# A spectral layer's filter loaded in long rows, with the columns kept in natural order by a strided matmul read, and another order of the first loads

## The chip, the cores and the metric

The kernel runs on one core of one Trainium2 chip, in one launch. The metric is the device time of an execution in microseconds (us), a median over runs. All arithmetic on the matrix engine (TensorE, PE in the profile) is in bf16 with f32 sums.

## What is computed

The input x is 2048 x 512 (bf16). The first half of the layer is a spectral filter, the second a token-mixing MLP:

```python
X  = rfft2(layernorm(x))                 # over both axes: 2048 x 257 complex
h  = x + irfft2(X * (w_r + 1j * w_i))    # w_r, w_i: 2048 x 257 each
g  = layernorm(layernorm(h))             # over the 512 columns
u  = gelu(einsum("sd,sf->df", g, w1) + b1)      # w1: 2048 x 1376
out = h + transpose(einsum("df,fs->ds", u, w2) + b2)
```

## The kernel before, in words

Token n is 16 * n1 + n2: n1 lies on the 128 partitions, n2 counts 16 tiles of 128 x 512. Both Fourier transforms are done as matmuls, the long one in two factors (128 and 16). The stages, with the names that the profile shows:

1. **Head and f1.** x is loaded in pieces (tile `X`), and the 16 slices of the first DFT factor, `FP`, in four pieces. Each x tile gets its mean and variance: tiles 1 and 3 by two passes on ScalarE (ACT; `JK<-X` in the profile, `nm` and `bv` on GpSimd, then `rs` on ACT), the others by `bn_stats` on VectorE (DVE, line 655), then `rs` on ACT. `fs_op` (lines 629 to 636) scales a slice of `FP` by `rs` into `FS`; GpSimd (POOL) does nine of them, ACT three, DVE four. 64 matmuls `ps<-FS,X` follow; their results are copied to `Y`, 13 by ACT and 3 by DVE (lines 692 to 696). 20 filler matmuls on zeros (`warm`, line 623) stand at the start of PE and 12 more between these.
2. **The filter.** Eight units u = 0..7. In each, eight `f2` matmuls (`ps<-EM,Y`, the DFT over the 512 columns), two copies to `CS` on ACT, eight `x` matmuls (`ps<-CS,EM`, the 16-point factor, in two row halves of 64), then on DVE one multiply by the filter (`V<-ps,W`, line 741; in units 0 and 7 two halves), then 16 `g1` matmuls (`ps<-EM,V`) and two copies to `PQ` on ACT. In `g1` V is the stationary operand, which PE loads (LDWEIGHTS, "PEld" in the profile), and a constant moves.
3. **Back.** `g2` and `g3` matmuls per x tile, then DVE adds x (lines 792, 794, 801) and normalises (`HH`, line 806); the first W1 matmuls run in between.
4. **MLP.** W1 matmuls, gelu on ACT, W2 matmuls (line 829, whose weight loads read every 16th column of W2), final add on DVE and stores.

The `W` tile holds the two filters for 32 groups of columns' frequencies: on each partition, `[group, w_r or w_i, 257]`. A partition is numbered by `_row`: four rows, two signs by two components (real and imaginary part), for each of 32 residues. Both components need the same filter row, and the row of the negative sign runs through the groups in falling order.

The 256 columns that stage 2 treats are frequencies 1 to 256, and `f2` makes the odd ones (par 0) and the even ones (par 1) as two blocks of 128. Before the change these blocks stay apart through `x`, and the multiply reads W with a step of two elements to match them; `g1` then takes `V[:, g, w, par * NP:par * NP + NP]`.

The order on each engine is not written out by hand: every operation is given to `K.op` with its engine, an estimated duration and a priority, and `Builder.schedule` places the ready operation that can start earliest. The resulting order of each engine is fixed at build time; at run time semaphores hold an instruction until what it needs is there. `schedule` also has a small model of the landing times of DMAs (lines 331 to 334), which the change alters, so orders can move on several engines. Loads are issued by SyncE (SP) on one queue, some by ACT on its own. The loads of W come in three parts, for unit 0, units 1 to 3 and units 4 to 7 (lines 583 to 600); a V multiply waits for all the loads of its part. The loads of W1 wait until the last part of W has landed.

Two small things belong to the order of the first loads before the change: a DMA of 64 bytes (`touch`) as the first one on ACT's queue, and a memset (`gate`) that the load of FP piece 0 waits for.

Of the kernel before, what the change touches and what calls it, by code (L numbers as in the profile page):

```python
# [34 lines left out]


def _row(sign, comp, k2, s):
    return 4 * (k2 * 2 + s) + 2 * sign + comp


def _fwd_matrices(special):
# [133 lines left out]
class Builder:  # L175
# [101 lines left out]
    def schedule(self):  # L277
        ops = self.ops
        eng_free = {s: 0.0 for s in _STREAMS}
        dma_free = 0.0  # L280
        bank_unit = [None] * PSUM_BANKS
        bank_free = [0.0] * PSUM_BANKS
        bank_last = [[] for _ in range(PSUM_BANKS)]
        open_cls = {}
        remaining = {o.idx: len(o.deps) for o in ops}
        inner = {o.idx: sum(1 for d, _ in o.deps if d.unit is not None and d.unit is o.unit) for o in ops}
        for o in ops:
            o.dep_ready = 0.0
        ready = [o for o in ops if remaining[o.idx] == 0]
        streams = {s: [] for s in _STREAMS}  # L290
        order = []
        while len(order) < len(ops):
            best = None
            for o in ready:
                bank, avail = None, 0.0
                u = o.unit
                if u is not None and not u.claimed:
                    if not o.first or open_cls.get(u.cls, 0) >= self.limits.get(u.cls, 8):
                        continue
                    if not u.early and any(remaining[x.idx] > inner[x.idx] for x in u.ops if x.pw):  # L300
                        continue
                    cand = None
                    for b in range(PSUM_BANKS - u.nbanks + 1):
                        if all(bank_unit[i] is None for i in range(b, b + u.nbanks)):
                            t = max(bank_free[b:b + u.nbanks])
                            if cand is None or t < cand[0]:
                                cand = (t, b)
                    if cand is None:
                        continue
                    avail, bank = cand  # L310
                st = max(eng_free[o.stream], o.dep_ready, avail, o.not_before)
                key = (st, -o.prio, o.idx)
                if best is None or key < best[0]:
                    best = (key, o, st, bank)
            assert best is not None, [(o.name) for o in ready][:20]
            _, o, st, bank = best
            e = o.stream
            ready.remove(o)
            o.sched, o.start = True, st
            if not o.is_dma:  # L320
                o.lane = e
            if bank is not None:
                u = o.unit
                u.claimed, u.bank = True, bank
                open_cls[u.cls] = open_cls.get(u.cls, 0) + 1
                for b in range(bank, bank + u.nbanks):
                    bank_unit[b] = u
                    for prev in bank_last[b]:
                        o.deps.append((prev, True))
            eng_free[e] = st + o.occ  # L330
            if o.is_dma:
                x0 = max(st + (1750.0 if st < 900.0 else 2200.0), dma_free)
                dma_free = x0 + o.bytes / (min(o.rate, 310.0) if x0 < 7000.0 else o.rate)
                o.finish = dma_free + 200.0
            else:
                o.finish = st + o.lat
            streams[e].append(o)
            order.append(o)
            if o.unit is not None and o.last:
                u = o.unit  # L340
                open_cls[u.cls] -= 1
                for b in range(u.bank, u.bank + u.nbanks):
                    bank_unit[b] = None
                    bank_free[b] = o.finish
                    bank_last[b] = [x for x in u.ops if x.pr]
            for c in o.consumers:
                if c.sched:
                    continue
                need = any(d is o and n for d, n in c.deps)
                c.dep_ready = max(c.dep_ready, o.finish if need else st + o.occ)  # L350
                remaining[c.idx] -= 1
                if remaining[c.idx] == 0:
                    ready.append(c)
        self.order, self.streams = order, streams
# [68 lines left out]
def memory_layout():  # L423
# [23 lines left out]
    add("CS", [NP, 16, 2, 2, NP], bf, rd)  # L447
    add("H", [NP, NS2, D_LEN], bf, rd)
    rw = region(2 * NG * LW * 2)
    add("W", [NP, NG, 2, LW], bf, rw)  # L450
    add("HH", [NP, NS2, D_LEN], bf, rw)
    rv = region(32768)
    add("V", [NP, NG, 2, 256], bf, rv)
# [16 lines left out]
    add("ZT", [NP, D_LEN], bf, region(1024))  # L470
    add("bv", [NP, NS2], f32, region(64))
    add("tb", [NP, 8], f32, region(32))
    add("pt", [NP, 32], bf, region(64))
    add("B1s", [NP, 16], bf, region(32))
    add("B1f", [NP, 16], f32, region(64))
    add("B2s", [NP, NS2], bf, region(32))
# [15 lines left out]
def build_kernel(nc, A_x, A_w_r, A_w_i, B_w1, B_b1, B_w2, B_b2, out):  # L492
# [65 lines left out]
    def ldx(a, b, pr_):  # L558
        dma(f"ld_x{a}", X[:, a:b, :], x_psd[:, a:b, :], (b - a) << 17, outs=[X[:, a:b, :]], prio=pr_)

    def ldf(q, pr_, stream="sp", nb=0.0, after=()):
        sl = slice(4 * q, 4 * q + 4)
        dma(f"ld_FP{q}", FP[:, sl, :, :], cin["FP"][:, sl, :, :], 1 << 18, outs=[FP[:, sl, :, :]], prio=pr_, stream=stream, not_before=nb, after=after)

    ZT, BV = T["ZT"], T["bv"]
    K.op("zt", "dve", lambda eng, bank: eng.memset(ZT[:, :], 0.0), outs=[ZT[:, :]], occ=200.0, prio=60)  # L566
    gate = K.op("gate", "dve", lambda eng, bank: eng.memset(T["TT0"][:, :, :], 0.0), outs=[T["TT0"][:, :, :]], occ=560.0, prio=59)
    for q, (a, b) in enumerate(((0, 1), (1, 2), (2, 4), (4, 6))):
        ldx(a, b, 96 - q)
    ldf(1, 88)  # L570
    ldx(6, 8, 87)
    ldx(8, 10, 86)
    ldx(10, 12, 85)
    ldf(2, 84)
    ldx(12, 16, 83)
    ldf(3, 82)
    act("table", T["tb"][:, 0:1], EPS[:, 0:1], ACT.Abs_reciprocal_sqrt, 1, ins=[EPS[:, 0:1]], prio=95)
    dma("touch", T["pt"][0:1, :], cin["FP"][0:1, 0, 0, 0:32], 64, outs=[T["pt"][0:1, :]], prio=99, stream="act")
    ldf(0, 90, "act", after=[gate])
    dma("ld_E", EM[:, 0:1024], cin["EM"][:, 0:1024], 1 << 18, outs=[EM[:, 0:1024]], prio=44)  # L580
    dma("ld_MR", EM[:, 1024:2048], cin["EM"][:, 1024:2048], 1 << 18, outs=[EM[:, 1024:2048]], prio=43)
    wload = {}
    for ch, (u0, u1) in enumerate(((0, 1), (1, 4), (4, 8))):
        g0, ng = 4 * u0, 4 * (u1 - u0)
        lst = []
        for w, dram in ((0, A_w_r), (1, A_w_i)):
            for comp in range(2):
                d = W[comp::4, g0:g0 + ng, w, :]
                lst.append(dma(f"ld_wp{ch}_{w}{comp}", d, bass.AP(dram.tensor, g0 * LW, [[64 * LW, 32], [LW, ng], [1, LW]]),
                               32 * ng * 514, prio=42 - ch, group=f"w{ch}", rate=300.0))  # L590
                h0, nh = (g0, ng) if g0 else (1, ng - 1)
                d = W[2 + comp::4, h0:h0 + nh, w, :]
                lst.append(dma(f"ld_wm{ch}_{w}{comp}", d, bass.AP(dram.tensor, (64 - h0) * LW, [[64 * LW, 32], [-LW, nh], [1, LW]]),
                               32 * nh * 514, prio=42 - ch, group=f"w{ch}", rate=300.0))
                if g0 == 0:
                    d = W[2 + comp::4, 0, w, :]
                    lst.append(dma(f"ld_wz{ch}_{w}{comp}", d, bass.AP(dram.tensor, 32 * LW, [[64 * LW, 32], [1, LW]]),
                                   32 * 514, prio=42 - ch, group=f"w{ch}", rate=300.0))
        for u in range(u0, u1):
            wload[u] = lst  # L600
    dma("ld_D2", EM[:, 2048:3072], cin["EM"][:, 2048:3072], 1 << 18, outs=[EM[:, 2048:3072]], prio=30)
# [14 lines left out]
    def junk():  # L616
        njk[0] += 1
        return JK[njk[0] % 4]

    wu = PsumUnit("warm", 1, early=True)  # L620

    def warm(name, unit, prio, after=(), first=False, last=False, occ=216.0):
# [95 lines left out]
    def stage_x(u):  # L718
# [3 lines left out]
        for i in range(2):  # L722
            G = 2 * u + i
            for c in range(2):
                for r in range(2):
                    rows = slice(64 * r, 64 * r + 64)
                    mm(f"x_{G}_{c}{r}", lambda bank, r=r, i=i: ps[:, bank + r, i * 256:i * 256 + 256],
                       M[rows, 1 if G == 0 and r == 0 else 0, c, :], CS[rows, G, :, c, :], unit, c == 0, c == 1, first, 13, 256, half=True, after=grp)
                    first, grp = False, ()
        g0 = 4 * u  # L730
        nh = 2 if u in V_SPLIT else 1
        ng = 4 // nh
        for h in range(nh):
            wt = W[:, g0 + h * ng:g0 + h * ng + ng, :, :]
            win = bass.AP(wt.tensor, wt.offset + 1, [list(wt.ap[0]), [LW, 2 * ng], [1, 2], [2, NP]])
            vout = V[:, g0 + h * ng:g0 + h * ng + ng, :, :].rearrange("p g w l -> p (g w l)")

            def tt(eng, bank, h=h, win=win, vout=vout):
# [8 lines left out]
    def stage_g1(u):  # L747
        for h in range(2):
# [4 lines left out]
            for gi in range(2):  # L753
                g = 4 * u + 2 * h + gi
                for par in range(2):
                    for w in range(2):
                        lastg1[0] = mm(f"g1_{g}_{par}{w}", lambda bank, gi=gi, par=par: ps[:, bank, gi * 256 + par * 128:gi * 256 + par * 128 + 128],
                           V[:, g, w, par * NP:par * NP + NP], R[:, 1 if g == 0 else 0, w, :], unit, w == 0, w == 1,
                           gi == 0 and par == 0 and w == 0 and not nw, 12, 128)
            g0 = 4 * u + 2 * h  # L760
            dst = PQ[:, :, :, :, 4 * g0:4 * g0 + 8].rearrange("p y q n (g k) -> p (y q n) g k", k=4)
# [72 lines left out]

    K.schedule()
    K.gen_sync()
    K.emit(es, ["dq_st", "dq_touch"] + [f"dq_st_{s2}" for s2 in range(NS2 - 2, NS2)])
    es.__exit__(None, None, None)
    return K

# [42 lines left out]
```

## Time and profile before

| | us |
|---|---|
| median of 3 runs (lowest to highest) | 137.02 (136.76 to 137.05) |
| the profiled execution | 136.76 |
| its span, first to last instruction | 135.0 |

| busy in that span | us | share |
|---|---|---|
| PE, matmuls | 124.9 | 93% |
| PE, weight loads (beside them) | 75.0 | 56% |
| DVE | 70.0 | 52% |
| ACT | 63.5 | 47% |
| POOL | 12.3 | 9% |

The stages in the span: first f1 matmul 8.5, first f2 matmul 21.3, first V multiply 24.15, end of the last about 42, first W1 matmul 49.9, last store's add 131.8. In profile lines, L is the line of the kernel before; a line that a helper records (528 for matmuls, 546 for ACT, 518 for DMAs) is told apart by its tiles. "[0.67 <-POOL bv L644]" means that the engine was idle for 0.67 us and that this instruction ended the wait. A matmul's length in the profile contains its pipeline, so what a matmul costs is read from the next one's start. The granted TensorE clock was 1.00 over the span.

### The profile page before, as it was taken

To read this page: it belongs to the slowest core of one execution; us is meant where nothing else is said; L and a number is where in the kernel's file an instruction comes from. 1 tells how busy PE (TensorE), PEld (TensorE's weight loads), DVE (VectorE), ACT (ScalarE), POOL (GpSimd) and SP (SyncE) were. 2 spreads that over 40 slices of the span, in tenths; PEclk is the share of its full clock that TensorE was granted. 3 is DMA by queue.
4 is the path that set the end of the run, shared out by engine and by line. 5 is a ranking of instruction groups with operands and counts; after the bars stand their busy time and mean duration, and the time that the engine had idled before them with its cause. 6 is when DMAs were issued, how large, how long until landed. Compare 5 with 4: busy or idle time off the path is not lost.

```text
span 135.0 us, 2023 instructions
## 1 busy us (share of the span) xinstructions
PE 124.9 (93%) x776; PEld 75.0 (56%) x786; DVE 70.0 (52%) x128; ACT 63.5 (47%) x146; POOL 12.3 (9%) x33
## 2 busy tenths in 40 slices
PE   6959988999986979999999999999999999999990
PEld 2315755678764845654434444456666666666660
DVE  2279694899994599999991000000233242322322
ACT  4457995688876999996679622222000000000000
POOL 0069890000100000000000000000000000000000
PEclk9999999999999999999999999999999999999999
DMA  4999589999999999995000000000011212112121
GB/s 97 238 375 395 139 210 252 296 294 317 323 427 434 419 398 408 418 342 155 0 0 0 0 0 0 5 0 0 9 68 39 78 39 76 45 39 78 39 78 41
DMA packets 16939, 22.17 MB, mean 164 GB/s; under 512 B 2754, under 2 KB 13250, under 8 KB 16418
## 3 DMA queue, kind: packets, MB, share of 16 engines
q1 hardware_dynamic: 16784, 21.79, 48.0%
q10 hardware_dynamic: 146, 0.26, 1.0%
q8 instruction: 6, 0.10, 0.3%
q14 instruction: 3, 0.02, 0.1%
HBM read 19.95 MB, written 2.10 MB: 163 GB/s over the span
## 4 chain that ended last, share of the span: by engine, by line
PE 56%; DVE 32%; DMA 4%; POOL 2%; ACT 1%; issue 1%; ACTq 0%; DVEq 0%; POOLq 0%
PE ps L528 54%; DVE V L741 12%; DVE H L801 7%; DMA FP<-c_FP 4%; DVE TT L792 4%; DVE TT L794 4%; DVE HH L806 4%; PE ps L623 2%; POOL FS L635 1%; DVE OUT L831 1%; DVE Y L694 1%; ACT PQ L546 0%; ACT Y L546 0%; ACTq L518 0%; ACT L546 0%
## 5 line engine op out<-in xcount | busy, mean ns | idle before, releaser
L528 PE MATMUL ps<-HH,W 128*128 128x512 bf16 (+1 forms) x173 | 40.4, 380 | 1.3 <-DVE HH L806 0.9
L528 PE MATMUL ps<-GT,W 128*128 128x512 bf16 (+1 forms) x172 | 37.9, 380 | 0.2
L831 DVE SCALAR_TENSOR_TENSOR OUT<-ps,B2f,H 128x512 bf16<-128x512 f32 x16 | 12.0, 751 | 48.7 <-PE ps L528 48.7
L528 PEld LDWEIGHTS ps<-GT,W 128*128 128x128 bf16 (+1 forms) x176 | 25.3, 144 | 12.8
L528 PEld LDWEIGHTS ps<-HH,W 128*128 128x128 bf16 (+1 forms) x176 | 17.2, 100 | 21.2 <-DVE HH L806 1.9
L741 DVE TENSOR_TENSOR V<-ps,W 128x2048 bf16<-128x2048 f32 (+1 forms) x10 | 17.8, 1856 | 0.9 <-PE ps L528 0.9
L546 ACT ACTIVATE GT<-ps,B1f 128x512 bf16<-128x512 f32 (+1 forms) x11 | 7.1, 688 | 14.6 <-PE ps L528 14.6
L546 ACT ACTIVATE JK<-H,nm 128x512 bf16<-128x512 bf16 x16 | 11.6, 722 | 3.0 <-DVE H L801 2.9
L623 PE MATMUL ps<-ZT 128*128 128x512 bf16 x32 | 10.9, 479 | 1.5 <-DVE ZT L566 1.2
L655 DVE BATCH_NORM_STATS2 st<-X 128x6 f32<-128x512 bf16 x14 | 9.1, 668 | 5.0 <-DMA X<-in_A_x_dram 5.0
L801 DVE TENSOR_TENSOR H<-ps,TT 128x512 bf16<-128x512 f32 x16 | 11.0, 685 | 0.0
L546 ACT ACTIVATE PQ<-ps 128x512 bf16<-128x512 f32 x16 | 9.1, 601 | 3.5 <-PE ps L528 3.1
L528 PE MATMUL ps<-FS,X 128*128 128x256 bf16 x64 | 8.5, 274 | 2.0 <-POOL FS L635 1.6
L528 PE MATMUL ps<-EM,V 128*128 128x128 bf16 x128 | 9.3, 220 | 0.4 <-DVE V L741 0.4
L528 PE MATMUL ps<-EM,PQ 128*128 128x256 bf16 x64 | 9.0, 273 | 0.8 <-ACT PQ L546 0.7
L546 ACT ACTIVATE EO<-ps 128x512 bf16<-128x512 f32 x16 | 9.2, 596 | 0.9 <-PE ps L528 0.9
L546 ACT ACTIVATE CS<-ps 128x512 bf16<-128x512 f32 x15 | 8.3, 607 | 2.0 <-PE ps L528 2.0
L528 PEld LDWEIGHTS ps<-EM,V 128*128 128x128 bf16 x128 | 7.5, 98 | 2.5 <-issue 1.7
L528 PE MATMUL ps<-EM,Y 128*128 128x256 bf16 x64 | 8.4, 273 | 0.5 <-ACT Y L546 0.5
L635 POOL TENSOR_SCALAR FS<-FP,rs 128x256 bf16<-128x256 bf16 x9 | 8.4, 943 | 4.0 <-DMA FP<-c_FP 2.8
L528 PEld LDWEIGHTS ps<-FS,X 128*128 128x128 bf16 x64 | 5.6, 98 | 5.5 <-POOL FS L635 3.5
L792 DVE TENSOR_TENSOR TT<-ps,X 128x256 f32<-128x256 f32 x16 | 6.7, 420 | 3.3 <-PE ps L528 3.3
(37 smaller groups left out, 81.2 us busy)
## 6 DMA issues: line engine op xcount, KB each, us to landing
W<-in_B_w_dram SPq DMA_DIRECT2D x4, 1376.0 KB, 11.1
W<-in_B_w_dram SPq DMA_DIRECT2D x10, 512.0 KB, 17.8
out_dram<-OUT SPq DMA_DIRECT2D x16, 128.0 KB, 1.7
X<-in_A_x_dram SPq DMA_DIRECT2D x5, 256.0 KB, 6.5
W<-in_A_w_r_dram SPq DMA_DIRECT2D x4, 257.0 KB, 4.8
W<-in_A_w_i_dram SPq DMA_DIRECT2D x4, 257.0 KB, 5.0
W<-in_A_w_r_dram SPq DMA_DIRECT2D x4, 192.8 KB, 3.2
W<-in_A_w_i_dram SPq DMA_DIRECT2D x4, 192.8 KB, 3.7
```

Source lines behind the costliest of these rows:

```text
L528: return K.op(name, "pe", lambda eng, bank: eng.matmul(outf(bank), lhsT, rhs, start=start, stop=stop), ins=ins or [lhsT, rhs], occ=occ, la ...
L546: return eng.activation(dst, s, func, **kw)
L623: return K.op(name, "pe", lambda eng, bank: eng.matmul(ps[:, bank, :], ZT[:, 0:NP], ZT[:, :], start=True, stop=True), ins=[ZT[:, :]], occ= ...
L635: dve(f"fs{i}", lambda eng, bank: eng.tensor_scalar(FS[:, i, :, :], FP[:, i, :, :], rs, None, op0=ALU.mult), [FP[:, i, :, :], rs], [FS[:, ...
L655: dve(f"st_{i}", lambda eng, bank, i=i, x=x: eng.bn_stats(ST[:, i, 0:6], x), [x], [ST[:, i, 0:6]], 512, prio=25)
L694: dve(f"y_{q}_{b}", lambda eng, bank, dst=dst, src=src: eng.tensor_copy(dst, src(bank)), [], [dst], 512, unit=unit, prio=28)
L741: return eng.tensor_tensor(vout, s, win, ALU.mult)
L792: dve(f"tl_{s2}", lambda eng, bank, tt=tt, xl=xl: eng.tensor_tensor(tt[:, 0, :], ps[:, bank, 256:512], xl, ALU.add), [xl], [tt[:, 0, :]], ...
L794: dve(f"th_{s2}", lambda eng, bank, tt=tt, xh=xh: eng.tensor_tensor(tt[:, 1, :], xh, ps[:, bank, 256:512], ALU.subtract), [xh], [tt[:, 1, ...
L801: return eng.tensor_tensor(hs.rearrange("p (h d) -> p h d", h=2), e, tt[:, :, :], ALU.add)
L806: dve(f"hh_{s2}", lambda eng, bank, s2=s2, hs=hs: eng.tensor_scalar(HH[:, s2, :], hs, NM[:, s2:s2 + 1], R2[:, s2:s2 + 1], op0=ALU.add, op1 ...
L831: dve(f"fin{s2}", lambda eng, bank, dst=dst, bia=bia, hs=hs: eng.scalar_tensor_tensor(dst, ps[:, bank, :], bia, hs, op0=ALU.add, op1=ALU.add),
```

## The change

Four things, which belong together or came together:

- **W in another layout.** `_row` swaps the places of sign and component, and `W` becomes `[w_r or w_i, group, 257]` on each partition. The rows of the positive sign are then every second partition, and a part's groups are contiguous in memory and in the tile: one transfer for both components (the source row is read twice), with one run of 4, 12 or 16 times 514 bytes for each partition. The negative sign still comes in rows of 514 bytes.
- **Columns in natural order.** So that W can be read without a step, the moving operand of `x` is read as (column, block): one element from the odd block, one from the even block, 512 bytes apart, in turn. V is then in natural order, and `g1` takes every second column of it, `V[:, g, w, par::2]`.
- **Another order of the first loads.** x tiles in pieces 0-2, 2-4, 4-6, 6-8, 8-12, 12-16 in place of 0, 1, 2-4, 4-6, 6-8, 8-10, 10-12, 12-16; FP pieces 0 and 1 from ACT's queue, without `touch` and `gate`.
- **Other constants in the schedule's model of DMA landings.**

In the built programs, PE has the same instructions; in f1 the fillers stand at other places, and between the `x` matmuls of units 5 and 6 there are 16 `g1` and 2 `f2` where there were 11 `g1`. The head of DVE, ACT and POOL is reordered: on POOL `bv` of tile 1 comes before the first FS, on ACT both passes over tile 1 before `rs` of tile 0, and `rs` of tile 1 before the passes over tile 3. On POOL the casts of b1 and b2 come after the first `nm` of line 661, not after all eleven. SP issues 20 loads of W where it issued 28.

```diff
 def _row(sign, comp, k2, s):
-    return 4 * (k2 * 2 + s) + 2 * sign + comp
+    return 4 * (k2 * 2 + s) + 2 * comp + sign
...
-                x0 = max(st + (1750.0 if st < 900.0 else 2200.0), dma_free)
-                dma_free = x0 + o.bytes / (min(o.rate, 310.0) if x0 < 7000.0 else o.rate)
+                x0 = max(st + (3200.0 if st < 4000.0 else 1700.0), dma_free)
+                dma_free = x0 + o.bytes / o.rate
...
-    add("W", [NP, NG, 2, LW], bf, rw)
+    add("W", [NP, 2, NG, LW], bf, rw)
...
-    gate = K.op("gate", "dve", lambda eng, bank: eng.memset(T["TT0"][:, :, :], 0.0), outs=[T["TT0"][:, :, :]], occ=560.0, prio=59)
-    for q, (a, b) in enumerate(((0, 1), (1, 2), (2, 4), (4, 6))):
-        ldx(a, b, 96 - q)
-    ldf(1, 88)
-    ldx(6, 8, 87)
-    ldx(8, 10, 86)
-    ldx(10, 12, 85)
+    for q, (a, b) in enumerate(((0, 2), (2, 4), (4, 6), (6, 8), (8, 12))):
+        ldx(a, b, 90 - q)
...
-    dma("touch", T["pt"][0:1, :], cin["FP"][0:1, 0, 0, 0:32], 64, outs=[T["pt"][0:1, :]], prio=99, stream="act")
-    ldf(0, 90, "act", after=[gate])
+    ldf(0, 90, "act")
+    ldf(1, 87, "act", 1800.0)
...
         for w, dram in ((0, A_w_r), (1, A_w_i)):
+            d = W[0:NP:2, w, g0:g0 + ng, :].rearrange("p g l -> p (g l)")
+            lst.append(dma(f"ld_wp{ch}_{w}", d, bass.AP(dram.tensor, g0 * LW, [[64 * LW, 32], [0, 2], [1, ng * LW]]),
+                           64 * ng * 514, prio=42 - ch, group=f"w{ch}"))
             for comp in range(2):
-                d = W[comp::4, g0:g0 + ng, w, :]
-                lst.append(dma(f"ld_wp{ch}_{w}{comp}", d, bass.AP(dram.tensor, g0 * LW, [[64 * LW, 32], [LW, ng], [1, LW]]),
-                               32 * ng * 514, prio=42 - ch, group=f"w{ch}", rate=300.0))
...
-                d = W[2 + comp::4, h0:h0 + nh, w, :]
+                d = W[1 + 2 * comp::4, w, h0:h0 + nh, :]
...
-                       M[rows, 1 if G == 0 and r == 0 else 0, c, :], CS[rows, G, :, c, :], unit, c == 0, c == 1, first, 13, 256, half=True, after=grp)
+                       M[rows, 1 if G == 0 and r == 0 else 0, c, :], CS[rows, G, :, c, :].rearrange("p y j -> p j y"), unit, c == 0, c == 1, first, 13, 256, half=True, after=grp)
...
-            win = bass.AP(wt.tensor, wt.offset + 1, [list(wt.ap[0]), [LW, 2 * ng], [1, 2], [2, NP]])
+            win = bass.AP(wt.tensor, wt.offset + 1, [list(wt.ap[0]), [LW, ng], [NG * LW, 2], [1, 256]])
...
-                           V[:, g, w, par * NP:par * NP + NP], R[:, 1 if g == 0 else 0, w, :], unit, w == 0, w == 1,
+                           V[:, g, w, par::2], R[:, 1 if g == 0 else 0, w, :], unit, w == 0, w == 1,
```

More of the change, by code (lines that the diff above doesn't have):

```diff
@@ L472, in memory_layout @@
     add("tb", [NP, 8], f32, region(32))
-    add("pt", [NP, 32], bf, region(64))
     add("B1s", [NP, 16], bf, region(32))
@@ L559, in ldx, with ldf @@
         dma(f"ld_x{a}", X[:, a:b, :], x_psd[:, a:b, :], (b - a) << 17, outs=[X[:, a:b, :]], prio=pr_)
-    def ldf(q, pr_, stream="sp", nb=0.0, after=()):
+    def ldf(q, pr_, stream="sp", nb=0.0):
         sl = slice(4 * q, 4 * q + 4)
-        dma(f"ld_FP{q}", FP[:, sl, :, :], cin["FP"][:, sl, :, :], 1 << 18, outs=[FP[:, sl, :, :]], prio=pr_, stream=stream, not_before=nb, after=after)
-    ZT, BV = T["ZT"], T["bv"]
-    K.op("zt", "dve", lambda eng, bank: eng.memset(ZT[:, :], 0.0), outs=[ZT[:, :]], occ=200.0, prio=60)
-    gate = K.op("gate", "dve", lambda eng, bank: eng.memset(T["TT0"][:, :, :], 0.0), outs=[T["TT0"][:, :, :]], occ=560.0, prio=59)
-    for q, (a, b) in enumerate(((0, 1), (1, 2), (2, 4), (4, 6))):
-        ldx(a, b, 96 - q)
-    ldf(1, 88)
-    ldx(6, 8, 87)
-    ldx(8, 10, 86)
-    ldx(10, 12, 85)
+        dma(f"ld_FP{q}", FP[:, sl, :, :], cin["FP"][:, sl, :, :], 1 << 18, outs=[FP[:, sl, :, :]], prio=pr_, stream=stream, not_before=nb)
+    for q, (a, b) in enumerate(((0, 2), (2, 4), (4, 6), (6, 8), (8, 12))):
+        ldx(a, b, 90 - q)
     ldf(2, 84)
@@ L576, in build_kernel @@
     ldf(3, 82)
-    act("table", T["tb"][:, 0:1], EPS[:, 0:1], ACT.Abs_reciprocal_sqrt, 1, ins=[EPS[:, 0:1]], prio=95)
-    dma("touch", T["pt"][0:1, :], cin["FP"][0:1, 0, 0, 0:32], 64, outs=[T["pt"][0:1, :]], prio=99, stream="act")
-    ldf(0, 90, "act", after=[gate])
+    ldf(0, 90, "act")
+    act("table", T["tb"][:, 0:1], EPS[:, 0:1], ACT.Abs_reciprocal_sqrt, 1, ins=[EPS[:, 0:1]], prio=88)
+    ldf(1, 87, "act", 1800.0)
     dma("ld_E", EM[:, 0:1024], cin["EM"][:, 0:1024], 1 << 18, outs=[EM[:, 0:1024]], prio=44)
@@ L586, in build_kernel @@
         for w, dram in ((0, A_w_r), (1, A_w_i)):
+            d = W[0:NP:2, w, g0:g0 + ng, :].rearrange("p g l -> p (g l)")
+            lst.append(dma(f"ld_wp{ch}_{w}", d, bass.AP(dram.tensor, g0 * LW, [[64 * LW, 32], [0, 2], [1, ng * LW]]),
+                           64 * ng * 514, prio=42 - ch, group=f"w{ch}"))
+            h0, nh = (g0, ng) if g0 else (1, ng - 1)
             for comp in range(2):
-                d = W[comp::4, g0:g0 + ng, w, :]
-                lst.append(dma(f"ld_wp{ch}_{w}{comp}", d, bass.AP(dram.tensor, g0 * LW, [[64 * LW, 32], [LW, ng], [1, LW]]),
-                               32 * ng * 514, prio=42 - ch, group=f"w{ch}", rate=300.0))
-                h0, nh = (g0, ng) if g0 else (1, ng - 1)
-                d = W[2 + comp::4, h0:h0 + nh, w, :]
+                d = W[1 + 2 * comp::4, w, h0:h0 + nh, :]
                 lst.append(dma(f"ld_wm{ch}_{w}{comp}", d, bass.AP(dram.tensor, (64 - h0) * LW, [[64 * LW, 32], [-LW, nh], [1, LW]]),
                                32 * nh * 514, prio=42 - ch, group=f"w{ch}", rate=300.0))
[L595 to L598, printed above, removed]
+            if g0 == 0:
+                d = W[1:NP:2, w, 0, :]
+                lst.append(dma(f"ld_wz{ch}_{w}", d, bass.AP(dram.tensor, 32 * LW, [[64 * LW, 32], [0, 2], [1, LW]]),
+                               64 * 514, prio=42 - ch, group=f"w{ch}", rate=300.0))
         for u in range(u0, u1):
@@ L618, in junk @@
         return JK[njk[0] % 4]
+    ZT, BV = T["ZT"], T["bv"]
+    K.op("zt", "dve", lambda eng, bank: eng.memset(ZT[:, :], 0.0), outs=[ZT[:, :]], occ=200.0, prio=60)
     wu = PsumUnit("warm", 1, early=True)
@@ L733, in stage_x @@
         for h in range(nh):
-            wt = W[:, g0 + h * ng:g0 + h * ng + ng, :, :]
-            win = bass.AP(wt.tensor, wt.offset + 1, [list(wt.ap[0]), [LW, 2 * ng], [1, 2], [2, NP]])
+            wt = W[:, :, g0 + h * ng:g0 + h * ng + ng, :]
+            win = bass.AP(wt.tensor, wt.offset + 1, [list(wt.ap[0]), [LW, ng], [NG * LW, 2], [1, 256]])
             vout = V[:, g0 + h * ng:g0 + h * ng + ng, :, :].rearrange("p g w l -> p (g w l)")
@@ L836, in build_kernel @@
     K.gen_sync()
-    K.emit(es, ["dq_st", "dq_touch"] + [f"dq_st_{s2}" for s2 in range(NS2 - 2, NS2)])
+    K.emit(es, ["dq_st"] + [f"dq_st_{s2}" for s2 in range(NS2 - 2, NS2)])
     es.__exit__(None, None, None)
```

## The prediction

> **What bounds the kernel now.** I read the page's chain of waits first (DVE V, line 741, holds 12% of the span and stage 1 ends in a mixture of engines), then the chain in order of time, then the timeline of the two stretches that the change touches. The sum is made against the profiled execution's own 136.76 us (its span is 135.0, so 1.76 lies outside); the median shown is 137.02, or 0.26 above.
>
> Stage 1, from the timeline (start, length, engine, what, idle time before and who ended it):
>
> ```profile
> 7.51 0.94 POOL L635 TENSOR_SCALAR FS<-FP,rs 128x256 bf16<-128x256 bf16 x1 [2.82 <-DMA FP<-c_FP]
> 7.54 0.63 ACT L546 ACTIVATE JK<-X 128x512 bf16<-128x512 bf16 x1 [2.33 <-DMA X<-in_A_x_dram]
> 8.55 0.29 POOL L644 TENSOR_SCALAR bv<-nm 128x1 f32<-128x1 f32 x1
> 8.94 0.29 ACT L546 ACTIVATE rs<-v,bv 128x1 f32<-128x1 f32 x1 [0.67 <-POOL bv L644]
> 10.62 2.77 POOL L635 TENSOR_SCALAR FS<-FP,rs 128x256 bf16<-128x256 bf16 x3
> 10.75 0.29 ACT L546 ACTIVATE rs<-v,bv 128x1 f32<-128x1 f32 x1 [0.72 <-POOL bv L644]
> ```
>
> Everything stands still until x tiles 2 and 3 and the first filter rows arrive at 7.5. Then ACT waits twice for `bv`, which is queued on POOL behind an FS of 0.94. After 10.75 ACT has no idle time over 0.21 until 20.06, so ACT carries stage 1 to its end.
>
> Stage 2, the multiply by W, from the timeline of DVE and PE and the chain in order of time:
>
> ```profile
> 23.40 0.61 PE L528 MATMUL ps<-CS,EM 64*128 64x256 bf16 x8
> 23.94 0.61 PE L528 MATMUL ps<-EM,Y 128*128 128x256 bf16 x4
> 24.15 1.04 DVE V L741
> 25.29 15.54 DVE V L741 x8
> 33.70 0.61 PE L528 MATMUL ps<-CS,EM 64*128 64x256 bf16 x8
> 35.21 2.28 DVE L741 TENSOR_TENSOR V<-ps,W 128x2048 bf16<-128x2048 f32 x1
> 36.30 0.61 PE L528 MATMUL ps<-CS,EM 64*128 64x256 bf16 x8
> 37.41 2.28 DVE L741 TENSOR_TENSOR V<-ps,W 128x2048 bf16<-128x2048 f32 x1
> ```
>
> DVE runs V without a gap from 24.15 to 41.95: a new one each 2.20 us. The eight x matmuls of a unit take 0.54 us (23.40 to the next start, 23.94): they run in pairs on two row halves, four pairs. V follows the end of x by 0.21 (24.15 less 23.94). Slack of x before its V, by the starts in the timeline: unit 5 ends at 34.24 and V starts at 35.21, so 0.76; unit 6 0.35 (36.85 to 37.41); unit 7 0.37 (39.02 to 39.60). PE is thus almost as full as DVE here. After V the rest follows in the same order, so a shift of the end of V is a shift of the kernel.
>
> **The change part by part.**
>
> *Head (issue order).* X0 and X1 come as one 256 KB transfer, FP0 is issued on ACT's queue at once in place of the 64-byte touch and behind the gate memset, FP1 moves to ACT's queue behind the activation-table load; SP loses three issues of about 0.4 us. X0+X1 now shares the engines with FP0: against landings of 3.4 and 3.7 I estimate 4.8 (its 256 KB and as much of FP0, at the 238 GB/s of the page's second slice, in place of 256 KB). This costs nothing: ACT sat idle from 5.2 to 7.54. FP0, no longer behind the gate, should land by 5.5 to 6.5 in place of 7.3. POOL's order now has `bv` of tile 1 ahead of the first FS, and ACT's has rs of tile 1 ahead of tile 3, so the first wait of 0.67 goes. Worked with X2-3 at 7.5 as before: ACT passes over tile 3 from 7.5 to 8.95 (0.72 each), POOL does `nm` of tile 3 at 8.3, FS1 8.5 to 9.45 and `bv` to 9.8, so rs of tile 3 stands at 9.85 in place of 10.75, with rs of tile 4 (0.2) already done. What is late next: X2-3, then ACT's own list, then x tiles 12 to 15, whose landing near 12.7 (issue at 5.76, 7.0 in flight) does not move, as the bytes ahead of it are the same; all of rs12 and later waits for that. Gain with X2-3 at 7.5: 0.9 + 0.2, about 1; if it lands 1 us earlier, up to 2; if it lands 1 us later (FP0 and FP1 take their share ahead of it, 256 KB more at about 400 GB/s is 0.6), a loss of up to 0.5. I take -1.0, range -2.0 to +0.5.
>
> *W loads.* 28 issues become 20, and the + half travels in rows of 2 to 8 KB instead of 514 B. In the page's slices the 514 B stretch moves 210 to 317 GB/s and the long-row stretch after it 398 to 434. Worth nothing by itself: the last W load of units 4 to 7 is issued at 27.03 and lands 5.4 later, at 32.4, 0.6 before V of unit 4 at 33.01. It is cover: with a head 1.0 us earlier, V of unit 4 would otherwise wait 0.4. Behind them on SP's queue come D2, IF, b1, b2, W1 and W2; all go earlier, and their users (first W1 matmul at 49.90) were not waiting. On POOL the casts of b1 and b2 now stand ahead of 10 of the 11 `nm` operations of line 661; they waited until 35.6 for their DMA, and the first user of those `nm` is after 48, so that is hidden.
>
> *V's read of W* goes from a step of 4 bytes to contiguous. V takes 2.20 us for 2048 elements, and H (line 801, everything in f32) 0.60 for 512 in the chain: 1.07 and 1.17 ns an element, whatever the steps. I take 0; a gain would need a faster mode with an f32 PSUM operand, which no row shows.
>
> *Moving read of x.* Now successive columns alternate between two places 512 B apart. No matmul of the trace has such a moving read. All contiguous ones of 256 columns start 0.109 us apart, so below nothing is excluded. The nearest row is a weight load with large steps: line 829 reads every 16th column of W2 (32 B apart):
>
> ```profile
> L528 PEld LDWEIGHTS ps<-GT,W 128*128 128x128 bf16 x160 | 23.0, 144 | 11.6
> L528 PEld LDWEIGHTS ps<-HH,W 128*128 128x128 bf16 x160 | 15.3, 98 | 19.7 <-DVE HH L806 1.9 <-issue 1.3
> ```
>
> The strided load takes 46 ns more for 128 columns. It costs nothing there (matmuls of 512 columns hide it), but the x matmul is itself the reader. At 46 ns per 128 columns a pair of 256 goes from 0.109 to 0.201, a unit from 0.54 to 0.91. Bounds: 0 and a doubling (0.44 a unit). I take 0.37.
>
> [...]
>
> *Weight load of g1.* V is now read at every second column (4 bytes). Its 128 loads of 98 ns run in step with matmuls 56 ns apart (eight in 0.45). Bounds 0 and 46 ns each; 4 bytes is nearer to 2 than to 32, so I take 0.
>
> *What x costs on the path.* V of unit 0 starts 0.37 later, and the V chain with it. Units 1 to 4 have slack of 0.87 to 2.1 against PE's growing delay. By the end of x of unit 5 PE has lost 6 x 0.37 = 2.2 and won back some 0.2 of idle; less the 0.76 of slack V of unit 5 starts about 1.3 late in all, the 0.37 of unit 0 included. Unit 6: before, x6 started 2.06 after x5 ended; the new order of PE puts 16 g1 and two f2 there instead of 11 g1, so 28 x 0.056 + 7 x 0.109 = 2.33, and with 0.91 for x6 itself V6 follows V5 by 3.24, not 2.20: 1.04 more. Unit 7 then has only two f2 and 10 g1 in front (0.8) and keeps up. End of V: +1.3 + 1.04 = +2.4 (at a doubling of x +2.8).
>
> Sum: 136.76 - 1.0 + 2.4 = 138.2.
>
> **Rivals.**
> 1. *The strided moving read is free, the head gives its microsecond* (ends faster): 136.76 - 1.0 = 135.8, 134.8 to 137.0. For it: a moving stream could be fetched ahead better than weights are. Against: the 144 ns row. It decides if x units stay below about 0.65 us, where the slack of units 6 and 7 still covers them.
> 2. *Also the 4-byte weight load of g1 is slow* (slower by much): 46 ns x 90 loads ahead of x7 on a PE that is by then the bound is +4.1, and the last 8 g1 +0.4: 138.2 + 4.5 = 142.7. Against: 4 bytes is far from 32.
> 3. *The head gains nothing*, because X2-3 lands at 8.0 or later behind FP0 and FP1, and x is free: 136.8 to 137.3.
>
> **How the numbers follow.** Main forecast 0.62 (own range 136.9 to 139.7 from head and x bounds), rival 1 0.24, rival 2 0.09, rival 3 0.05. 0.2% (0.27 us) is about what can be told from no change here. Slower: 0.58 of the main case, 0.03 of rival 1, 0.09, 0.03, so 0.73; faster: 0.19 of rival 1 and 0.02 of the main case, 0.21; same 0.06. Range 135.6 to 140.2: outside it lie rival 2, the best third of rival 1 and a little of the main case's upper end.
>
> **What would show it.** x units: eight CS,EM matmuls followed by the next start after 0.9 us (mine) or 0.54 (rival 1); pairs 0.2 or 0.11 apart. V with gaps that PE ends, from unit 3 or 5 on, and 19.8 us from first V to last end in place of 17.8. EM,V weight loads near 98 ns (144 would be rival 2). First f2 matmul at about 20.3 in place of 21.34, FS at 7.0 in place of 7.51. W landing by 28. My prediction is wrong if V stays without a gap, or if stage 1 ends later than 21.8.

## The result, and the profile after

| | before | changed |
|---|---|---|
| median of 4 runs (lowest to highest), us | 136.89 (136.71 to 137.05) | 138.43 (138.37 to 138.50) |
| the profiled execution, us | 136.76 | 138.37 |
| its span, us | 135.0 | 136.4 |

The ratio is 1.0113, 95% interval 1.0095 to 1.013: slower by 1.3 to 1.8 us. The forecast was 138.2 us and "slower". The total was right to 0.2 us by luck: the two large terms behind it were both too small, and their errors cancelled. Where runs of a kernel lie more than 1.5% above its fastest, the medians below contain them and the ratios do not.

The start of the first f2 matmul before, and stage 1 of the changed kernel, both from timelines:

```profile
21.34 2.13 PE L528 MATMUL ps<-EM,Y 128*128 128x256 bf16 x17 [0.47 <-ACT Y L546]
```

```profile
4.91 0.63 ACT L545 ACTIVATE JK<-X 128x512 bf16<-128x512 bf16 x1 [2.30 <-DMA X<-in_A_x_dram]
6.18 0.69 DVE L649 BATCH_NORM_STATS2 st<-X 128x6 f32<-128x512 bf16 x1 [0.36 <-DMA X<-in_A_x_dram]
6.53 0.95 POOL L629 TENSOR_SCALAR FS<-FP,rs 128x256 bf16<-128x256 bf16 x1 [0.21 <-ACT rs L545]
8.77 0.29 ACT L545 ACTIVATE rs<-mv,eps 128x1 f32<-128x1 f32 x1 [0.83 <-DVE mv L650]
9.43 0.29 ACT L545 ACTIVATE rs<-mv,eps 128x1 f32<-128x1 f32 x1 [0.37 <-DVE mv L650]
9.63 0.28 ACT L545 ACTIVATE rs<-v,bv 128x1 f32<-128x1 f32 x1
19.13 2.08 PE L527 MATMUL ps<-EM,Y 128*128 128x256 bf16 x16 [0.41 <-ACT Y L545]
```

x tiles 0 and 1 are there at 4.9 (3.4 and 3.7 before), tiles 2 and 3 at 6.2 (7.5 before), the first FS starts at 6.53 (7.51), the rs of tile 3 stands at 9.63 (10.75), and the first f2 matmul comes at 19.13 in place of 21.34: stage 1 is 2.2 us shorter.

Stage 2, from the timeline of DVE before and those of PE and DVE in the changed kernel:

```profile
24.15 17.81 DVE L741 TENSOR_TENSOR V<-ps,W 128x1024 bf16<-128x1024 f32 x10 [0.93 <-PE ps L528]
```

```profile
21.25 1.14 PE L527 MATMUL ps<-CS,EM 64*128 64x256 bf16 x8
22.32 0.61 PE L527 MATMUL ps<-EM,Y 128*128 128x256 bf16 x4
22.53 6.75 DVE L735 TENSOR_TENSOR V<-ps,W 128x1024 bf16<-128x1024 f32 x4 [1.47 <-PE ps L527]
29.84 4.49 DVE L735 TENSOR_TENSOR V<-ps,W 128x2048 bf16<-128x2048 f32 x2 [0.56 <-PE ps L527]
35.41 2.29 DVE L735 TENSOR_TENSOR V<-ps,W 128x2048 bf16<-128x2048 f32 x1 [1.08 <-PE ps L527]
39.04 4.55 DVE L735 TENSOR_TENSOR V<-ps,W 128x2048 bf16<-128x2048 f32 x3 [1.34 <-PE ps L527]
```

Eight x matmuls now take 1.07 us to the next start (21.25 to 22.32) where they took 0.54; in the trace their pairs start 0.243 us apart, not 0.109. V, without a gap before, now waits for PE in units 3, 5 and 6 (0.56, 1.08 and 1.34), each time for the x of its unit. It ends at 43.60 in place of 41.95: 24.47 after the first f2 matmul, where it was 20.61. So stage 2 lost 3.86 and stage 1 gave 2.21; 1.65 remains, and the rest of the kernel is shifted by it (first g2 matmul 45.02 for 43.38). The two other prices taken as nothing in stage 2 were nothing: V comes every 2.2 us where it doesn't wait, with contiguous reads of W as with stepped ones, and the weight loads of g1 from every second column take what they took (first before, then changed):

```profile
L528 PEld LDWEIGHTS ps<-EM,V 128*128 128x128 bf16 x128 | 7.5, 98 | 2.5 <-issue 1.7 <-DVE V L741 0.7
L527 PEld LDWEIGHTS ps<-EM,V 128*128 128x128 bf16 x128 | 7.6, 98 | 3.0 <-issue 2.7 <-DVE V L735 0.3
```

### The profile page after: what moved, and what is told of

Read it like the earlier page. It is cut to its first block, busy times and chain, and to the rows that moved or that the text cites. A ratio compares the mean times of both kernels' runs of the same rounds, so it can differ in the third digit from the quotient of the medians.

```text
span 136.4 us, 2005 instructions
## 1 busy us (share of the span) xinstructions
PE 128.6 (94%) x776; PEld 75.2 (55%) x786; DVE 69.4 (51%) x127; ACT 63.3 (46%) x146; POOL 12.2 (9%) x33
## 4 chain that ended last, share of the span: by engine, by line
PE 60%; DVE 23%; ACT 9%; DMA 5%; issue 1%; SPq 1%; ACTq 0%
PE ps L527 60%; DVE H L795 7%; ACT Y L545 5%; DMA X<-in_A_x_dram 5%; DVE TT L786 4%; DVE TT L788 4%; DVE HH L800 4%; DVE V L735 3%; ACT rs L545 1%; ACT PQ L545 1%; ACT FS L545 1%; DVE st L649 1%; ACT CS L545 1%; SPq L517 1%; DVE OUT L825 1%
## 5 line engine op out<-in xcount | busy, mean ns | idle before, releaser
L527 PE MATMUL ps<-CS,EM 64*128 64x256 bf16 x64 | 9.1, 404 | 0.2
```

What stands on the lines that cost most here:

```text
L527: return K.op(name, "pe", lambda eng, bank: eng.matmul(outf(bank), lhsT, rhs, start=start, stop=stop), ins=ins or [lhsT, rhs], occ=occ, la ...
```

## The experiments

The theory after the result: the head is worth -2.2 us, the strided moving read about +3.9, and the long rows of W nothing beyond what V would have waited for. The rivals: the loss is in the new order of PE, in g1's weight step or in W's layout; the head's gain comes from W's long rows. Ratios are to the kernel before on the same chip, with the 95% interval.

### One part at a time

**e1: the changed head alone.** Loads of x and FP and the model of landings as changed; W, x and g1 as before.

> The kernel before with the head of the changed kernel alone (order of the first loads and the model of landings); W in its old layout, 28 issues of 514 B rows, x read contiguously. Theory (the head is worth 2.2 us, the strided x read costs about 3.9): first f2 matmul at 19.1 as in the changed kernel, V without gaps, 134.7 us, unless the last W load (32.4 before) now holds V of unit 4, wanted at 30.8: then up to 1 us of it comes back, 135.7. Rival (the head's gain came from the long rows of W, which leave the queue sooner): f2 at 21.3, 136.9.

134.58 us, 0.9815 (0.9784 to 0.9846). First f2 matmul at 19.27; V has no gap but 0.06 us at unit 6. The last W load lands at 30.26, before V of unit 4 at 31.00, although its rows are the old ones: three issues fewer stand ahead of the loads of W on SP's queue, the first of them is issued at 5.79 and not at 8.02, the last at 25.16 and not at 27.03. The whole gain is in the head, and nothing of it comes from the long rows.

**e2 and e11: the strided read alone.** The same kernel twice.

```diff
-   CS[rows, G, :, c, :]
+   CS[rows, G, :, c, :].rearrange("p y j -> p j y")
-   [list(wt.ap[0]), [LW, 2 * ng], [1, 2], [2, NP]]
+   [list(wt.ap[0]), [LW, 2 * ng], [1, 256]]
-   V[:, g, w, par * NP:par * NP + NP]
+   V[:, g, w, par::2]
```

> The kernel before with the strided moving read of x alone: V in natural order, W in its old layout and with its old loads but read without the step of two, g1 on every second column; order on PE as before. Theory: x pairs 0.243 us apart, units of 1.07, gaps in V from unit 3 on, end of V 3.4 to 3.9 later, 140.3 to 140.8 us. Rival (the loss is that of the new PE order at units 5 and 6, of g1's weight step or of W's layout, and x has little to do with it): under 138 us.

> The strided moving read of x alone once more (same kernel as e2_stride), since the clock was down to 0.66 for some microseconds of stage 1 in that profile. Theory: with the full clock first f2 matmul at 21.3 as before, V ending 24.4 after it in place of 20.6, about 140.5 us. Rival (part of the 24.4 came from the disturbed clock): under 23.8.

e2: 141.06 us, 1.0213 (1.016 to 1.0265); in its profile the granted clock was 0.66 between 10 and 15 us, and the first f2 matmul came at 22.49 (21.58 in e11). e11: 140.19 us, 1.0255 (1.0202 to 1.0308). All waits of V in stage 2 of e11:

```profile
DVE V L741 <- PE ps L528: 4.4, 5, 1.5
```

That is 1.47 before the first V, 0.54 more than before, and 0.56, 1.08, 0.85 and 0.41 before units 3, 5, 6 and 7. V ends 24.42 us after the first f2 matmul in both profiles, so the lower clock in stage 1 had no part in it. PE has the order of before here, with 11 g1 and not 16 ahead of x of unit 6, and the sum is the same as in the changed kernel (24.47): the new order only moved waits from unit 7 to unit 6. e1 shows the same from the other side: PE has the order of the changed kernel there, and without the strided read V has no gap over 0.06.

**e3: the long rows alone.** W's new layout and loads with the head of before. To keep x contiguous, the copy to CS makes the natural order; g1 reads every second column.

```diff
-   dst = CS[:, G, :, :, :].rearrange("p y c j -> p (y c j)")
+   dst = CS[:, G, :, :].rearrange("p c (j y) -> p y c j", y=2)
-   CS[rows, G, :, c, :].rearrange("p y j -> p j y")
+   CS[rows, G, c, :]
```

> The kernel before with W in long rows alone (new layout, 20 issues); the natural order of columns is made by the copy to CS (ACT writes with a step of 4 bytes), so that x reads contiguously; g1 on every second column as in the changed kernel; head as before. Theory: the last W load lands by 28 in place of 32.4, but nobody waited for it, so 136.9 us within 0.3; EM,V weight loads stay at 98 ns. Rival (traffic of long rows, or the 4-byte weight step, slows PE or DVE in the filter stage): V with gaps, over 137.5. Rival 2 (the ACT copy with a step of 4 bytes is slower than 0.6 us): CS copies over 0.7 us.

136.43 us, 0.9966 (0.9935 to 0.9996): a small gain at most. The last W load lands at 29.45 in place of 32.42, and V starts and ends as before (24.12, 41.93). Rival 2 was right in its number: the copies to CS take 0.75 us and not 0.60. Here that is hidden.

**e5: the changed kernel without the strided read.** The same copy, under the changed head.

> The changed kernel without its strided moving read: the copy to CS puts the columns in natural order (a step of 4 bytes in the write) and x reads contiguously; all else as changed. Theory: keeps the head's 2.2 us and loses the 3.9 us of the strided read: x pairs 0.109 us apart, V without a gap from about 22.0 to 39.8, 134.6 us, faster than both kernels. Rival (the loss sits elsewhere in the change): 137 us or more.

134.95 us, 0.9841 (0.981 to 0.9873). x pairs are 0.109 us apart again. V has one gap of 0.37, at unit 6: x waits for the slower copy there, as the row of the copy shows (least, median and longest in ns, against 592/597/645 before):

```profile
L545 ACT ACTIVATE CS<-ps x15: 724/751/789, 19.8 to 35.7; 128x512 bf16<-128x512 f32 x15
```

So e1 and e5 both beat both kernels, and e1, which leaves W and x as they were, is not behind.

### What the moving read costs

**e6: another step in each unit.**

```diff
+   X_STEP = {2: 1, 3: 2, 4: 4, 5: 8, 6: 16, 7: 64}
...
+   return cs.rearrange("p y (a b) -> p y b a", b=X_STEP[u])
```

> The changed kernel, but the moving read of x has another step in each unit: units 0 and 1 as changed (two places 512 bytes apart in turn), unit 2 contiguous, unit 3 a step of 4 bytes, unit 4 of 8, unit 5 of 16, unit 6 of 32, unit 7 of 128 bytes. From unit 2 on the columns meet other columns' filter values, so the output is not the reference's. [...] Rival 1 (any step other than 2 bytes is slow): 0.24 from unit 3 on. Rival 2 (only the turn between two far places is slow): 0.109 from unit 2 on.

One run, 138.69 us. From PE's timeline, x of units 2 to 7, each followed by the next group, so that the difference of the starts is the unit's time:

```profile
25.00 0.61 PE L527 MATMUL ps<-CS,EM 64*128 64x256 bf16 x8
25.54 0.62 PE L527 MATMUL ps<-EM,V 128*128 128x128 bf16 x8
...
27.84 0.63 PE L527 MATMUL ps<-CS,EM 64*128 64x256 bf16 x8
28.40 0.45 PE L527 MATMUL ps<-EM,V 128*128 128x128 bf16 x5
28.79 1.07 PE L527 MATMUL ps<-CS,EM 64*128 64x256 bf16 x8
29.79 1.68 PE L527 MATMUL ps<-EM,V 128*128 128x128 bf16 x27
...
32.83 1.96 PE L527 MATMUL ps<-CS,EM 64*128 64x256 bf16 x8
34.72 0.84 PE L527 MATMUL ps<-EM,V 128*128 128x128 bf16 x12
...
37.28 2.00 PE L527 MATMUL ps<-CS,EM 64*128 64x256 bf16 x8
39.21 0.39 PE L527 MATMUL ps<-EM,Y 128*128 128x256 bf16 x2
...
40.29 1.15 PE L527 MATMUL ps<-CS,EM 64*128 64x256 bf16 x8
41.37 1.82 PE L527 MATMUL ps<-EM,V 128*128 128x128 bf16 x24
```

| read of x | unit, us | pairs start apart, us |
|---|---|---|
| contiguous (2 bytes) | 0.54 | 0.109 |
| step of 4 bytes | 0.56 | 0.113 |
| step of 8 bytes | 1.00 | 0.227 |
| step of 16 bytes | 1.89 | 0.451 |
| step of 32 bytes | 1.93 | 0.460 |
| two places 128 bytes apart in turn | 1.08 | 0.244 |
| two places 512 bytes apart in turn | 1.07 | 0.242 |

Unit 7's "step of 128 bytes" is in fact a turn between two places, as only two such steps fit in a row. None of the expectations holds as written: a pair takes 4% more at a step of 4 bytes, twice as much at 8 (0.227 after 0.113) and twice that at 16 (0.451), and at 32 hardly more (0.460). The turn between two places costs about half of a step of 16 bytes, at 128 as at 512 bytes (0.244 and 0.242). What makes these prices, no run shows.

**e10: the natural order one step earlier**, by f2 writing PSUM with a step of two f32 elements; copy and x contiguous.

```diff
-   lambda bank, par=par: ps[:, bank, par * 256:par * 256 + 256]
+   lambda bank, par=par: ps[:, bank, :].rearrange("p (c j y) -> p y c j", c=2, y=2)[:, par]
```

> The changed kernel with natural order made one step earlier: the f2 matmuls write PSUM with a step of two f32 elements, so that the copy to CS and the read of x are both contiguous. Theory: CS copies back to 0.6 us from 0.75, x pairs 0.109; if PE writes PSUM with a step at full rate, f2 matmuls stay 0.109 apart and it is 0.1 to 0.4 us faster than the version with the ACT copy (134.6 us). Rival (a stepped write of PSUM is slow like the stepped read of SBUF): f2 matmuls 0.2 us apart, 64 of them, V with gaps, over 137 us.

140.93 us, 1.0311 (1.0276 to 1.0346): the rival. The first f2 matmuls of e10, and for comparison of e5:

```profile
19.04 3.84 PE L527 MATMUL ps<-EM,Y 128*128 128x256 bf16 x17 [0.41 <-ACT Y L545]
```

```profile
18.87 2.18 PE L527 MATMUL ps<-EM,Y 128*128 128x256 bf16 x17 [0.41 <-ACT Y L545]
```

From the second on they start 0.216 us apart and not 0.109. The copies to CS are back to 0.60 us, which doesn't help.

### Where the head's 2.2 us come from

**e9: the changed loads under the old model of landings**, which leaves the loads, SP and POOL as in e1 and changes the orders on ACT, DVE and PE.

> The loads of the changed head (as e1_head) under the old model of landings: the loads as in e1_head, POOL and SP in the same order, ACT, DVE and PE in another. Theory (landings make the gain): f2 at 19.1 to 19.5, 134.6 us. Rival (the order that goes with the new model makes half of it): f2 at 20.2 or later, over 135.4 us.

135.55 us, 0.9919 (0.989 to 0.9948): the rival. x tiles 2 and 3 land at 6.25 (6.35 in e1), and yet the first f2 matmul of e9 is 1.0 us behind that of e1, here in this order:

```profile
20.27 1.80 PE L528 MATMUL ps<-EM,Y 128*128 128x256 bf16 x14 [0.47 <-ACT Y L546]
```

```profile
19.27 2.18 PE L528 MATMUL ps<-EM,Y 128*128 128x256 bf16 x17 [0.42 <-ACT Y L546]
```

So of the 2.07 us from 21.34 to 19.27 the new loads alone make 1.07 and the order of the engines 1.0 more. The medians agree (135.55 and 134.58).

The landings themselves vary from run to run. With the first loads of before, tiles 2 and 3 landed between 6.9 and 7.7 in six profiles (before, e2, e3, e11, e12, e13), although SP's queue began alike in all (7.3 and 7.7 in e2 and e11, the same kernel); with the new ones between 6.0 and 6.35 (changed, e1, e5, e6, e9, e10). Half a microsecond between two profiles with the old loads need therefore not be the order's.

**e12: the changed model alone**, with the loads of before; **e13: e12 with W in long rows** as in e3.

> The kernel before with the changed model of landings alone: the same loads in the same order and queues, only the orders on POOL, ACT, PE and DVE change (bv of tiles 1 and 3 earlier on POOL, another place of the fillers on PE). Prediction's step (order alone is worth 0.9 to 1.1 with tiles 2 and 3 at 7.5): first f2 matmul at 20.3; then V of unit 4 waits for W, 136.3 us. Theory after the first runs (the head's gain is landings): f2 at 21.0 to 21.4, 136.8 us.

> The kernel of e12_order (old loads of x and FP, engine orders of the changed model) with W in long rows and the natural order made by the copy to CS, as in e3_longrows. Theory (the order is worth 1.0 to 1.4 us of stage 1, and with the old loads of W this is lost in V's wait for W): f2 at 20.0 to 20.4, no wait of V for W, 135.2 to 135.9 us. Rival (the order alone is worth nothing): 136.4 us or more, like e3_longrows.

e12: 137.23 us, 1.0022 (0.9995 to 1.005), and yet its first f2 matmul is at 19.98 (x tiles 2 and 3 landed at 6.9 in this run, 0.6 earlier than in the profile of before, so not all of the 1.36 is the order's). DVE's timeline shows where it went:

```profile
26.72 2.29 DVE L741 TENSOR_TENSOR V<-ps,W 128x2048 bf16<-128x2048 f32 x1 [1.52 <-DMA W<-in_A_w_i_dram]
```

V of unit 1 waits 1.52 us for W, and unit 4 waits 0.26 again: with the old loads of W an earlier end of stage 1 is given back. e13: 136.13 us, 0.9944 (0.9918 to 0.997); f2 at 19.48, no wait of V for W, and a gap of 0.39 at unit 6 as in e5. In this profile f2 is 1.83 earlier than in e3 (21.31), with tiles 2 and 3 landing 0.5 earlier. But the profiled execution took 135.55 us, and the median lies 0.2 above the expected range and only 0.3 under that of e3, with intervals that overlap. With the old loads, what the order is worth in the kernel's time stays open.

**e7: before without touch and gate; e8: before with x tiles 0 and 1 in one transfer.** Both change the engines' order too.

```diff
 e7
-   gate = K.op("gate", ...)
-   dma("touch", ..., stream="act")
-   ldf(0, 90, "act", after=[gate])
+   ldf(0, 99, "act")
 e8
-   for q, (a, b) in enumerate(((0, 1), (1, 2), (2, 4), (4, 6))):
+   for q, (a, b) in enumerate(((0, 2), (2, 4), (4, 6))):
```

> The kernel before without the touch and the gate: FP piece 0 is issued on ACT at once; x tiles 0 and 1 stay single transfers, FP piece 1 stays on SP. Theory (the head's 2.2 us are the earlier landing of FP0 and of x tiles 2 and 3, and these come from issuing more bytes earlier): FP0 lands by 5.5 in place of 7.3, first f2 matmul by 20.2 in place of 21.3, about 135.8 us. Rival (the single transfers of x are what holds tiles 2 and 3 back): FP0 early, tiles 2 and 3 still at 7.5, f2 at 20.8 to 21.3, over 136.4 us.

> The kernel before with x tiles 0 and 1 in one transfer, touch and gate kept. Theory: FP0 still lands late (about 7), so POOL's first FS and what follows stay near 7.3, f2 at 20.8 or later, over 136.3 us. Rival (the single transfers are what held tiles 2 and 3 back): tiles 2 and 3 land by 6.5, f2 by 20.2, 135.8 us or less.

e7: 136.07 us, 0.9947 (0.9905 to 0.9988). FP0 lands at 4.72, x tiles 2 and 3 at 5.76, f2 starts at 20.29; V of unit 1 then waits 1.2 us for W. (The profiled execution took 137.20 us, 1.1 above the median, so the usual wait may be shorter.) e8: 137.01 us, 1.0009 (0.9967 to 1.0051). FP0 stays at 7.04, x tiles 2 and 3 land at 4.33, f2 starts at 20.48, and V of unit 4 waits for W:

```profile
32.80 2.29 DVE L741 TENSOR_TENSOR V<-ps,W 128x2048 bf16<-128x2048 f32 x1 [0.56 <-DMA W<-in_A_w_i_dram]
```

So with either half of the change of the first loads, and the order that goes with it, tiles 2 and 3 come sooner and f2 is 0.9 to 1.05 earlier, and in both profiles W takes part of it back. In neither is W issued earlier: its first load goes out at 8.74 and 8.42 (8.02 before), its last lands at 33.40 and 32.78, although e8 has one issue fewer on SP's queue. Why tiles 2 and 3 of before land as late as 7.5 was not isolated further.

## Why the prediction was right or wrong

- **Head: direction right, size too small, path wrong.** It was the step "I take -1.0", which rests on x tiles 2 and 3 landing at 7.5 as before. They landed at 6.2, and -2.2 was measured, 0.2 outside the range given. The prediction had the case itself ("if it lands 1 us earlier, up to 2"), and that the order is worth about 1 us agrees with e9 against e1. But rs of tile 3, put at 9.85, stood at 9.63 by luck: with the earlier landing the same working gives 8.5. `bv` was done at 9.06, and ACT came to this rs only after those of tiles 2 and 4, which waited 0.83 and 0.37 for DVE. DVE's order puts the statistics of tile 4 ahead of what rs of tile 2 needs, and tiles 4 and 5 landed at 7.93. The other 1.1 us lie behind it: ACT then works without idle time up to f2, where before it waited 0.21 and 0.65 for PE. x tiles 12 to 15, said not to move from 12.7, landed at 11.73; ACT did not wait for them.
- **W in long rows: worth nothing by itself, right** to within the 0.7% that the interval of e3 leaves; V starts and ends as before. That it was needed as cover was half right: with the old loads of x ahead of it, W does hold V up once stage 1 ends earlier (e12, e7, e8). With the changed head it doesn't, because W is issued 2.2 us earlier and the last load lands at 30.26, before V wants it at 31.00 (e1). The prediction counted the three issues that leave SP's queue and did not carry them on to W's landing; e8 shows that the count alone does not tell the time of issue.
- **Moving read of x: direction right, price too small.** 0.37 us a unit was taken from the nearest row, a weight load with a step of 32 bytes; 0.53 was measured, above the upper bound of 0.44, which held a doubling for the worst. The step that failed is taking the weight load's difference for a moving read: the weight load loses 46 ns on 128 columns at 32 bytes (144 against 98), the moving read 0.35 us on 256 (0.460 against 0.109). At that step of 32 bytes a unit of x costs 1.39 more (e6), so that 0.37 came as near as it did is luck. The doubling, behind the 0.44 as behind the +2.8 at the end of V, was the author's estimate, and no run shows where it would come from. Measured, the turn took 2.2 times a contiguous pair (0.243 against 0.109 us), a step of 8 bytes 2.1 times (0.227) and one of 16 bytes 4.1 times (0.451).
- **What it costs on the path.** The walk gave +2.4 from +0.37 a unit; with 0.53 the same steps give 6 x 0.53 - 0.2 - 0.76 = 2.2 at unit 5 (2.4 measured) and, for unit 6, 1.2 more (1.43 measured, where the weight loads of x of unit 6 also waited 0.33 for its copy). The first gap, 0.56 at unit 3, follows from the same steps: 4 x 0.53 - 0.2 - 0.87 = 1.05, of which 0.53 is there since unit 0, so 0.52. The reason given for unit 6, the new order of PE, was wrong: with the old order the same loss falls on units 6 and 7 (e11), and with the new order and no strided read there is none (e1).
- **Weight load of g1 and V's read of W: nothing, right**, at 98 ns and 2.2 us.
- **The sum** of -1.0 and +2.4 stood for -2.2 and +3.86. Rivals 2 and 3 did not occur; rival 1 had the head's sign right, and e1 shows the kernel that it described, at 134.58 us just under the range given for it.

## What to carry to other kernels

A layout that makes a load or a multiply neater may have to be paid for where the order is turned round, and the price depends on who turns it: here the matrix engine's moving read cost 3.9 us, its write to PSUM more (ratio 1.0311 in e10, against 1.0113 for the changed kernel), the copy on ACT 0.15 us each (0.75 for 0.60, e5), and leaving it to the multiply nothing (a V every 2.2 us with either read of W). Before a transfer is made faster, look whether somebody waits for its landing, and whether the wait appears only once another stage is shortened. When a forecast adds two opposite terms, give each its own bounds from the right kind of row: a total that agrees says little of the terms.

## What the runs showed of the hardware that was not expected

- A bf16 moving read with a step of 4 bytes costs 4% (0.113 against 0.109 us for a pair of 256 columns), of 8 bytes 2.1 times, of 16 or 32 bytes 4.1 to 4.2 times; turning between two places 2.2 times (e6).
- A matmul that writes PSUM with a step of two f32 elements ran at half rate: one every 0.216 us for 256 columns (e10) against 0.109 without the step.
- ACT's copy of 128x512 elements from PSUM to bf16 takes 0.75 us with a step of 4 bytes in its write, 0.60 without (e5).
- With three issues fewer at the start of SP's queue, and other first loads, the first W load is issued 2.2 us earlier (5.79 for 8.02) and the last lands 2.2 us earlier (30.26 for 32.42, e1); with one fewer (e8) neither comes earlier (8.42 and 32.78).
- The same first loads, issued in the same order, landed x tiles 2 and 3 anywhere from 6.9 to 7.7 us in six profiles.
